# Decode attention, forward and backward: the output projection's load moved back in the load queue

## The chip, the cores and the metric

The kernel runs on one core of one Trainium2 chip. The metric is the device time of one execution in microseconds (us); smaller is better. "Before" and "after" are the kernel without and with the change.

## The reference

The program computes a small transformer block for two decode tokens and all its gradients. Cut to what matters, with B = 2 batches, H = 32 heads, 4096 cached keys of 128 numbers per head, and a model width of 640, all in bf16:

```
q   = layernorm(x) @ wq                     # 640 -> 32 heads x 128
p   = softmax(q . K / sqrt(128))            # per batch and head, over 4096 keys
o   = p @ V
h   = x + concat(o) @ wo                    # 4096 -> 640
out = h + relu(layernorm(h) @ w1) @ w2      # 640 -> 1728 -> 640
# and from grad_out: the gradients of x, K, V, wq, wo, w1, w2
```

The K and V caches are 2 x 32 tiles of 1 MB each, and the gradients of K and V have the same sizes and are written out. These 1 MB tiles are nearly all of the traffic; wo is 5 MB, wq 5 MB, w1 and w2 2 MB each.

## The kernel before, in words

**Two sweeps.** The first sweep (`p1_iter`, L463) goes through the 64 pairs of batch and head in order. In iteration i it transposes K tile i on TensorE (L416), copies the transposed groups out of PSUM, and takes the scores (L427). In the next iteration it finds the softmax's maximum (L517, L519) and exponentials (L526) for tile i and multiplies them into K (`pk_half`, L478). In the one after that it multiplies the result with V tile i (`m_part`, L471) and sums it over the keys (`u_part`, L500). So iteration i reads K tile i, K tile i-1 and V tile i-2. The second sweep (`p2_iter`, L834) reads V once more and writes the gradients of K and V, each as an outer product on VectorE (L829) that GpSimd's queue stores (L867, L886). From iteration 41 of the first sweep on, one iteration of the second sweep runs beside every second one of the first.

**Between the sweeps.** When the first batch's 32 heads are through, `middle_gen` (L730) is queued as background work at iteration 33. It finishes the output projection, runs the second layer norm, multiplies with w1 (`hf_ps`, L755), goes back through the MLP with w1 on VectorE (L789), and takes the gradient of the attention's output with wo on VectorE (`go_group`, L670). Pieces of it are woven into the first sweep's iterations. The second sweep needs its results.

**The output projection** runs in groups of four heads, eight groups for a batch. `o_group` (L593) normalises four heads' outputs on VectorE. `a_group` (L600) multiplies them with their rows of wo in 20 small TensorE matmuls (L606) and adds the result up on VectorE (L608). `a_heads(i)` (L611) is called once in each iteration, before step 5, and does one of the two: the product of a group that is normalised, or else the normalising of the next group, when its heads are through and, for the first batch, when the quarter of wo that it needs was queued at least four iterations before (L617). What is left at iteration 33 is done by `middle_gen`.

**The load queue.** All loads of the first sweep are issued by SyncE in one fixed order. It is written out before the kernel runs: for each iteration, in this order, a piece of wq (every sixth), K tile i, V tile i-2, a tile of the second sweep, and then what the two lists name for it: `W_AT` the four quarters of wo and w1 (`load_weights`, L344), `W2_AT` the three pieces of w2:

```python
W_AT = (10, 15, 20, 24, 35)
W2_AT = (8, 13, 18)
...
if ii in W_AT:
    queue.append(("w", W_AT.index(ii)))
```

`pump` (L1097) takes entries from the head of this queue as long as there is a buffer. K, V, wq and w2 come into twelve buffers of 1 MB; wo and w1 have homes of their own and need none. A load that takes over a buffer is issued when the last reader of the old tile is done. SyncE issues in order, so nothing passes an entry that waits. The queue runs some iterations ahead of the work, as far as the buffers go. V tiles of the last six heads of the first batch stay in their buffers for the second sweep.

The order on each engine is fixed when the program is built. TensorE, too, works strictly in order, so a product that waits for its weights holds up all that stands behind it.

Of the kernel before, what the change touches and what calls it, by code (L numbers as in the profile page):

```python
# [15 lines left out]
def kernel(  # L16
# [23 lines left out]
    _, H, Sk, Dh = A_k_cache.shape  # L40
# [14 lines left out]
    OG = 4  # L55
# [337 lines left out]
    NP1 = len(pairs)  # L393
# [193 lines left out]
        yield  # L587


    o_next = [0]  # L590
    a_next = [0]

    def o_group():  # L593
        b, g = divmod(o_next[0], H // OG)
        hs = slice(g * OG, g * OG + OG)
        nc.vector.tensor_tensor(out=OU[:, b, hs], in0=OU[:, b, hs], in1=rt[:, b, hs], op=ALU.mult)
        nc.vector.tensor_copy(out=OFc[:, hs, b], in_=OU[:, b, hs])
        o_next[0] += 1

    def a_group():  # L600

        b, g = divmod(a_next[0], H // OG)
        a_ps = pst([128, ND], FP32, "mid", "a_ps")
        for c in range(ND):
            for h in range(g * OG, g * OG + OG):
                nc.tensor.matmul(a_ps[:, c:c + 1], lhsT=wo_t[:, h, c * 128:(c + 1) * 128], rhs=OFc[:, h, b:b + 1],  # L606
                                 start=(h == g * OG), stop=(h == g * OG + OG - 1))
        nc.vector.tensor_tensor(out=asum[:, b, :], in0=asum[:, b, :], in1=a_ps[:], op=ALU.add)  # L608
        a_next[0] += 1

    def a_heads(i):  # L611

        if a_next[0] < o_next[0]:
            a_group()
        elif o_next[0] < NP1 // OG and i >= o_next[0] * OG + OG + 2:
            b, g = divmod(o_next[0], H // OG)
            if b > 0 or i >= W_AT[g * OG * 4 // H] + 4:  # L617
                o_group()

    def u_out(b):  # L620
# [447 lines left out]
    i = j = 0  # L1068
# [7 lines left out]


    queue = []
    W_AT = (10, 15, 20, 24, 35)
    W2_AT = (8, 13, 18)  # L1080
    for n, (ii, jj) in enumerate(plan):
        if ii is not None:
# [7 lines left out]
        if ahead is not None and ahead < NP1 and turns[ahead] not in kept and ("W", ahead) not in queue:  # L1090
            queue.append(("W", ahead))
        if ii in W_AT:
            queue.append(("w", W_AT.index(ii)))
        if ii in W2_AT:
# [35 lines left out]
    for n, (i, j) in enumerate(plan):  # L1130
# [58 lines left out]
        for k, _ in enumerate(p1_iter(i, i < H + 1, 0)):  # L1189
            for _ in range(at.get(k, 0)):  # L1190
                if g2 is not None:
                    p2_step()
            if k == 5:
                a_heads(i)
            pump()

            spread[0] = 1 if i < P2_AT else 2
            at_k[0] = k
            if i >= P2_AT:
                slot[0] = int(k == 6 or (k == 1 and j is None))  # L1200
            elif i > H + 1:
                slot[0] = {1: 2, 3: 1, 4: 1, 6: 1}.get(k, 0)
            else:
                slot[0] = int(k in (1, 6))
            bg_step(0, rate)
            bg_step(1, 0.0)
# [43 lines left out]
```

## Time and profile before

| | |
|---|---|
| median of 4 runs | 918.41 us (915.03 to 921.66) |
| the profiled execution | 918.38 us, span of the profile 916.5 us |
| busy share of the span | PE 82%, DVE 76%, ACT 58%, POOL 18% |
| DMA | 363.00 MB, 394 to 396 GB/s over the span |
| granted TensorE clock, mean over the span | 0.781 |
| K, V tile loads: issue to landing, median | 14.4 and 14.3 us (1024 KB) |
| a quarter of wo: issue to landing, median | 19.8 us (1280 KB, 4 loads) |
| w1: issue to landing | 11.2 us (2160 KB, 1 load) |

The profile shows one execution. PE is TensorE, PEld its weight loads, DVE is VectorE, ACT ScalarE, POOL GpSimd, SP SyncE; a name with a q (SPq) is the engine's own instruction queue, which issues DMAs. L471 is line 471 of the kernel. In lines with a time in front, the first number is the start in us from the span's start and the second how long it took; a bracket at the end tells how long the engine stood idle before it and what ended that. The name `w_t` stands for w1 and for the pieces of w2, with their numbers left out; w1 is the one of 2160 KB, issued by L349.

### The profile page before, as it was taken

What the parts mean: (1) busy time and instruction counts of PE and PEld (TensorE: products, weight loads), DVE (VectorE), ACT (ScalarE), POOL (GpSimd) and SP (SyncE); (2) the same over time, 40 slices, a digit from 0 to 9 for tenths busy, and PEclk for the clock granted to TensorE, in tenths of its full rate; (3) what the DMA queues carried; (4) which work ended last, traced back from release to release, by engine and by line L of the source; (5) the groups of instructions that cost most, each with busy time, mean ns of one, the idle gap of its engine ahead of it and who ended that gap; (6) DMA issues with size and microseconds to landing.
All of it is one profiled execution on the core that took longest, in us unless ns stands there. A gap on an engine that the chain in (4) does not pass through costs nothing.

```text
span 916.5 us, 26502 instructions
## 1 busy us (share of the span) xinstructions
PE 750.4 (82%) x11226; PEld 627.7 (68%) x11226; DVE 692.7 (76%) x1291; ACT 531.4 (58%) x1096; POOL 166.0 (18%) x329
## 2 busy tenths in 40 slices
PE   5998898999989898988887946866878799878493
PEld 5887786888878787877776835754657567555362
DVE  4655785877778887777768789977798359998875
ACT  3665564566777776776643535544656667566362
POOL 1222222223201101010011112111122011111111
PEclk9999998999999999999885576556655556565556
DMA  8999999998889999999999999999999999999997
GB/s 346 418 395 411 406 393 410 411 417 336 309 320 326 412 422 422 422 423 422 410 360 410 368 424 405 398 410 394 398 406 386 424 368 423 425 426 425 425 422 315
DMA packets 59478, 363.00 MB, mean 396 GB/s; under 512 B 5696, under 2 KB 15552, under 8 KB 19168
## 3 DMA queue, kind: packets, MB, share of 16 engines
q1 hardware_dynamic: 37920, 212.18, 58.3%
q0 software_dynamic: 18432, 134.23, 35.3%
q10 hardware_dynamic: 3008, 14.91, 4.1%
q8 instruction: 88, 1.44, 0.6%
q14 instruction: 30, 0.25, 0.1%
HBM read 212.16 MB, written 149.13 MB: 394 GB/s over the span
## 4 chain that ended last, share of the span: by engine, by line
PE 38%; DMA 27%; DVE 18%; ACT 8%; issue 7%; POOL 1%; POOLq 0%; SPq 0%; ACTq 0%; DVEq 0%
DMA out_dram<-gK 13%; DMA Vt<-in_A_v_cache_dram 11%; PE t_ps L437 8%; PE m_ps L471 8%; PE t_ps L416 7%; DVE gV L829 5%; DVE gK L829 4%; ACT t_sb L421 4%; PE s_ps L427 3%; DVE junk L656 3%; PE o_ps L933 3%; PE u_ps L500 2%; DVE pk L478 2%; DVE gxj L656 2%; PE dp_ps L450 2%
## 5 line engine op out<-in xcount | busy, mean ns | idle before, releaser
L421 ACT COPY t_sb<-t_ps 128x1024 bf16<-128x1024 bf16 x223 | 217.5, 1017 | 45.8 <-PE t_ps L416 45.6
L442 ACT COPY t_sb<-t_ps 128x512 f32<-128x512 f32 x256 | 149.9, 588 | 148.3 <-PE t_ps L437 144.3
L437 PE MATMUL t_ps<-ident_f,Wt 128*128 128x128 f32 x848 | 199.5, 384 | 1.6 <-ACT t_sb L421 1.6
L478 DVE TENSOR_TENSOR pk<-Kt,ep 128x2048 bf16<-128x2048 bf16 x128 | 156.3, 1221 | 57.7 <-ACT ep L526 25.5
L471 PE MATMUL m_ps<-pk,Vt 128*128 128x129 bf16 x2048 | 171.5, 222 | 17.6 <-DMA Vt<-in_A_v_cache_dram 16.5
L829 DVE TENSOR_TENSOR gK<-rb,gsp 128x2048 bf16<-128x2048 bf16 x128 | 152.1, 1223 | 21.1 <-DMA out_dram<-gK 18.7
L829 DVE TENSOR_TENSOR gV<-rb,pp 128x2048 bf16<-128x2048 bf16 x128 | 152.7, 1218 | 16.9 <-DMA out_dram<-gV 7.8
L416 PE MATMUL t_ps<-ident_bf,Kt 128*128 128x128 bf16 x2048 | 153.6, 224 | 10.2 <-DMA Kt<-in_A_k_cache_dram 5.0
L471 PEld LDWEIGHTS <-Vt 128*128 128x128 bf16 x2048 | 125.1, 99 | 48.7 <-issue 30.5
L437 PEld LDWEIGHTS t_ps<-ident_f,Wt 128*128 128x128 f32 x848 | 138.2, 199 | 28.1 <-issue 21.7
L416 PEld LDWEIGHTS <-Kt 128*128 128x128 bf16 x2048 | 126.0, 100 | 18.0 <-issue 9.0
L450 PEld LDWEIGHTS <-t_sb 128*128 128x128 bf16 x2048 | 96.6, 107 | 39.4 <-ACT t_sb L442 18.2
L450 PE MATMUL dp_ps<-gom,t_sb 128*128 128x2 bf16 x2048 | 95.6, 168 | 8.9 <-ACT t_sb L442 8.2
L488 POOL COPY pk<-ep 128x16 bf16<-128x16 bf16 x80 | 62.7, 785 | 194.2 <-ACT ep L526 162.1
L427 PE MATMUL s_ps<-qc,t_sb 128*128 128x1 bf16 x2048 | 88.1, 164 | 1.2 <-DVE t_sb L419 1.2
L867 POOL DMA_DIRECT2D out_dram<-gK x64 | 34.0, 532 | 278.2 <-DVE gK L829 209.6
L886 POOL DMA_DIRECT2D out_dram<-gV x64 | 34.2, 534 | 267.4 <-DVE gV L829 221.6
L939 ACT CAST ot<-o_ps 128x512 bf16<-128x512 f32 (+4 forms) x160 | 70.4, 488 | 17.2 <-DMA out_dram<-ot 8.7
L427 PEld LDWEIGHTS <-t_sb 128*128 128x128 bf16 x2048 | 77.7, 97 | 3.7 <-DVE t_sb L419 1.3
L583 ACT CAST MT<-m_ps 128x128 bf16<-128x128 f32 x64 | 17.1, 267 | 76.3 <-PE m_ps L471 76.2
L856 ACT ACTIVATE rb<-dp_ps,rt 128x256 bf16<-128x256 f32 x64 | 30.4, 475 | 51.3 <-PE dp_ps L851 50.6
L656 DVE CUSTOM_DVE_ANT_0 junk<-wo_t,hbc 128x640 bf16<-128x640 bf16 x64 | 52.3, 818 | 0.2
(194 smaller groups left out, 775.0 us busy)
## 6 DMA issues: line engine op xcount, KB each, us to landing
Kt<-in_A_k_cache_dram SPq DMA_DIRECT2D x64, 1024.0 KB, 14.4
Vt<-in_A_v_cache_dram SPq DMA_DIRECT2D x64, 1024.0 KB, 14.3
out_dram<-gV POOLq DMA_DIRECT2D x64, 1024.0 KB, 10.9
out_dram<-gK POOLq DMA_DIRECT2D x64, 1024.0 KB, 10.6
Wt<-in_A_v_cache_dram SPq DMA_DIRECT2D x53, 1024.0 KB, 12.1
wo_t<-in_A_wo_dram SPq DMA_DIRECT2D x4, 1280.0 KB, 19.8
wqs<-in_A_wq_dram SPq DMA_DIRECT2D x5, 1024.0 KB, 14.2
wq_t<-in_A_wq_dram SPq DMA_DIRECT2D x5, 960.0 KB, 11.1
```

The source lines that it names most:

```text
L416: nc.tensor.transpose(t_ps[:, j, :], nat[:, g * GT + j, :], ident_bf[:])
L421: nc.scalar.copy(out=t_sb[:], in_=t_ps[:])
L427: nc.tensor.matmul(dst[:, sc:sc + 1], lhsT=t_sb[:, j, :], rhs=vec, start=True, stop=True)
L437: nc.tensor.transpose(t_ps[:, j, :], natf[:, 2 * cc:2 * cc + 2, :].rearrange("p c k -> p (c k)"), ident_f[:])
L442: nc.scalar.copy(out=t_sb[:], in_=t_ps[:])
L450: nc.tensor.matmul(dst[:, sc:sc + 2], lhsT=v[:, j, :, par], rhs=vecs[:, par, :], start=(par == 0), stop=(par == 1))
L471: nc.tensor.matmul(r["m"][:, 0:129], lhsT=r["V"][:, sc, :], rhs=r["pk"][sc // HALF][:, sc % HALF, 0:129], start=(sc == 0), stop=(sc == NSC ...
L478: nc.vector.tensor_tensor(out=p["pk"][k][:, :, 0:128].rearrange("p s (a two) -> p s a two", two=2), in0=p["K"][:, sl, :].rearrange("p s (a ...
L488: nc.gpsimd.tensor_copy(out=col, in_=e)
L656: nc.vector.tensor_tensor_reduce(out=junk[0:kc, 0:width], in0=in0, in1=in1, scale=1.0, scalar=0.0, op0=ALU.mult, op1=ALU.add, accum_out=acc)
L829: nc.vector.tensor_tensor(out=pairs_view(dst[:, sl, :]), in0=row.rearrange("p (a two) -> p a two", two=2)[:, None, :, :].to_broadcast([128 ...
L939: nc.scalar.copy(out=ot[0:P, k, n0:n0 + nn], in_=o_ps[0:P, 0:nn])
```

## The change

It touches two places. In the list `W_AT`, the quarters of wo are named for iterations 14, 19, 28 and 33 instead of 10, 15, 20 and 24, and w1, the list's last entry, for 36 instead of 35. In `a_heads`, the normalising of a group (`o_group`) is no longer the alternative to a product (`a_group`): both may now run in the same iteration, first the product of the group before, then the normalising of the next. And the first iteration in which a quarter's groups may be normalised is now named in a list of its own, `WO_HERE`, instead of four after the quarter's place in the queue (16, 21, 29 and 31, where it was 14, 19, 24 and 28).

```diff
+    WO_HERE = (16, 21, 29, 31)
     o_next = [0]
     a_next = [0]
...
         if a_next[0] < o_next[0]:
             a_group()
-        elif o_next[0] < NP1 // OG and i >= o_next[0] * OG + OG + 2:
+        if o_next[0] < NP1 // OG and i >= o_next[0] * OG + OG + 2:
             b, g = divmod(o_next[0], H // OG)
-            if b > 0 or i >= W_AT[g * OG * 4 // H] + 4:
+            if b > 0 or i >= WO_HERE[g * OG * 4 // H]:
                 o_group()
...
-    W_AT = (10, 15, 20, 24, 35)
+    W_AT = (14, 19, 28, 33, 36)
     W2_AT = (8, 13, 18)
```

## The prediction

> **What bounds the kernel now.** I call iteration i of the first sweep "row i": it transposes K tile i and uses V tile i-2. I read the page's slices first, then stretches of 10 to 20 us, then the chain, then the two queues that matter, TensorE and SyncE.
>
> ```profile
> PEclk9999998999999999999885576556655556565556
> DMA  8999999998889999999999999999999999999997
> ```
>
> The DMA engines are full nearly everywhere, with one dip in slices 10 to 13. Stretches show where it starts (columns: PE, PEld, DVE, ACT, POOL busy, clock, DMA share, GB/s):
>
> ```profile
> 20.00:40.00 20.00, 19.16 (x370) 16.77 (x370) 12.07 (x20) 12.35 (x24) 4.06 (x11) 1.00 1.01 418
> 60.00:80.00 20.00, 16.22 (x297) 13.52 (x295) 10.01 (x15) 10.51 (x21) 4.27 (x7) 0.94 1.02 406
> 140.00:160.00 20.00, 16.93 (x295) 14.56 (x299) 11.07 (x23) 9.99 (x19) 4.98 (x7) 0.83 1.02 409
> 210.00:220.00 10.00, 9.74 (x191) 8.33 (x189) 6.00 (x9) 7.07 (x13) 3.89 (x5) 1.00 0.78 294
> 240.00:250.00 10.00, 8.79 (x176) 7.77 (x172) 9.90 (x25) 8.36 (x17) 1.61 (x4) 1.00 0.68 237
> 300.00:320.00 20.00, 17.64 (x330) 15.78 (x330) 16.81 (x28) 15.53 (x33) 2.77 (x4) 1.00 1.01 420
> ```
>
> Up to 210 us loads and TensorE are neck and neck: the queue is full, and TensorE mostly has 19 of 20 us. From 210 to 290 the engines set the pace and the queue has gaps. From 300 to 880 DMA is at 0.97 to 1.01, with nothing in hand to make a delay good. TensorE's rows show where loads come late before 210:
>
> ```profile
> 76.22 0.64 PE L471 MATMUL m_ps<-pk,Vt 128*128 128x129 bf16 x8 [2.91 <-DMA Vt<-in_A_v_cache_dram]
> 110.04 0.64 PE L471 MATMUL m_ps<-pk,Vt 128*128 128x129 bf16 x8 [1.37 <-DMA Vt<-in_A_v_cache_dram]
> 141.57 1.15 PE L416 MATMUL t_ps<-ident_bf,Kt 128*128 128x128 bf16 x16 [2.79 <-DMA Kt<-in_A_k_cache_dram]
> 144.06 1.05 PE L471 MATMUL m_ps<-pk,Vt 128*128 128x129 bf16 x8 [1.23 <-DMA Vt<-in_A_v_cache_dram]
> ```
>
> These are rows 11, 16 and 21, each shortly behind a quarter of wo. The last places are w1's load on SyncE, its size and time to landing, and its first reader on TensorE:
>
> ```profile
> 215.64 0.44 SPq L349 DMA_DIRECT2D w_t<-in_B_w_dram  x1
> 220.30 0.33 SPq L458 DMA_DIRECT2D Kt<-in_A_k_cache_dram  x1
> 226.42 0.33 SPq L458 DMA_DIRECT2D Vt<-in_A_v_cache_dram  x1
> 226.85 0.37 SPq L458 DMA_DIRECT2D Kt<-in_A_k_cache_dram  x1
> ```
>
> ```profile
> w_t<-in_B_w_dram SPq DMA_DIRECT2D x1, 2160.0 KB, 11.2
> ```
>
> ```profile
> 226.36 1.05 PE L416 MATMUL t_ps<-ident_bf,Kt 128*128 128x128 bf16 x16
> 231.02 0.89 PE L755 MATMUL hf_ps<-x2c,w_t 128*128 128x1 bf16 x30
> ```
>
> w1 is issued at 215.64, lands at 226.83 and is read at 231.02, in row 35, which starts at 226.36. It has 4.2 us in hand.
>
> **Quarters 0 to 2 of wo.** Landings (by the trace's DMA semaphores) follow the order of issue: K and V tiles land 2.49 us apart (141.52 and 144.01 for K21 and V19), and a quarter lands 3.51 us after the load ahead of it in three of four cases (once 5.21). A row without waits takes 5.51 us (89.30 to 94.81); every fourth takes 0.20 more, one with a piece of q 0.76 more (row 5: 6.27), one with a wo product 0.50 more (row 25: 6.01). Rows 11 to 23 took 162.66-72.19 = 90.5 us against 13x5.51+3x0.20+3x0.76+4x0.50 = 76.5, so 14.0 us went to late loads and to the half clock behind them.
>
> Quarter 0 moves behind V12 (past eight tiles and a piece of w2), quarter 1 from behind V13 to behind V17, quarter 2 from V18 to V26, quarter 3 from V22 to V31. In row 11, V9 lands at 76.17-3.51 = 72.66, and TensorE wants it at 73.14: no wait. TensorE then reaches row 15 at 72.19+6.27+5.71+5.51+5.51 = 95.19. But K15 and V13 have quarter 0 ahead of them before and after the change, so they land when they did, at 98.93 and 101.50: 5.4 us of wait come back here. Row 15 goes on at 101.54, as before. With the slow clock behind it (1.9, below) row 16 starts at 101.54+4.56+1.9 = 108.0 (before 107.55). K16 and V14 now have one quarter fewer ahead: no wait. Rows 16 to 20 take 5.71+6.77+6.01+5.51+5.71 = 29.7, to 137.7. K21 and V19 have two quarters ahead instead of three and land at 138.0 and 140.5: waits of 0.3 and 1.5, and row 21's V products start at 140.5 instead of 144.06. The first gain is one quarter, 3.5 us, plus up to 1.8 if the shorter waits bring no slow clock.
>
> **Quarter 3** is wanted by the product in row 32. It lands behind V31: 209.91-3.51+3.51 = 209.9. TensorE comes there at 208.91-3.5-0.5+5.28 = 210.2 (one wo product fewer stands before row 32), or 208.4 with the 1.8 above: a wait of 0 to 1.5. The next row starts at 209.9+0.94 = 210.9 to 211.1, not 214.62. So the gain at row 33 is 3.5 to 3.8; I take 3.7. If the 5.21 us were the quarter's true price, quarter 3 would land at 208.2 and the gain be 5.5. If one of the odd landing gaps of 1.5 (V9 came 4.03 after K11, K30 4.04 after V27) fell badly, it would be 2.0.
>
> **Products in neighbouring rows.** The eight products of the first half stay eight: rows 15, 17, 20, 22, 25, 27, 31, 34 become 17, 18, 22, 23, 30, 31, 32, 34, each 0.50 us of TensorE. Their three VectorE operations (0.15 to 0.17 us) move along, and VectorE has 6 to 8 of 20 us free in most of these stretches: nothing. From row 33 on, the order on the compute engines is unchanged.
>
> **w1, the last entry of the list, goes from row 35 to 36.** That moves its load past K36 and V34. V34 waits for VectorE's second product with K33, at the end of row 34, and so issues at row 35's start (226.42 against 226.36). w1 can't issue before it: 226.85 on the old scale, 0.5 into row 35. With the measured 11.19 it lands at 238.0, and TensorE wants it at 231.02: 7.0 us of wait. Everything behind that weight load on TensorE waits too: the rest of row 35's V products and scores, hence the maximum on VectorE and the exponential on ScalarE, and the MLP's whole chain to row 41. No transfer uses the time, since the tiles behind w1 need buffers that these rows free. Lower bound: V36 to V38 landed 4.7 to 5.0 after issue from an empty queue; with 5.0, and w1's 640 packets of 135 ns on 16 engines (5.4 us) behind, it lands at 236.8, a wait of 5.8. Upper: V34 landed 5.59 after issue and w1 6.53 after the load ahead: 238.5, a wait of 7.5. I take 7.0, w1's own row.
>
> The page "DMA: Bandwidth & Descriptors" of the Trainium skill, section on the anatomy of one DMA, gives about 2.0 us plus bytes at 436 GB/s: for V34 and w1 together, 3.26 MB, I estimate 9.5 us from V34's issue, 235.9, a wait of 4.9, and the sum below would be 2.1 us lower. Its rules for kernel authors say to issue a load early and wait late, which speaks against moving w1.
>
> **The clock behind waits.** After row 11's wait the clock averages 0.57 over 77 to 81 us and 0.53 over 142 to 149. From row 11's V products to row 12 it took 6.34 us instead of 5.32, and row 12 lost 1.03 more (together 2.05); row 21 lost 1.76. Row 16's short waits cost none. So 0 to 2.05 behind w1's wait; I take 1.8, as it is the longest of these waits. The skill's page "TensorE: Matmul & The Clock Gate", part 1, has half rate after an idle window of about 3.4 us until one busy window has passed; by that alone I estimate 1.7.
>
> **Sum.** 7.0 + 1.8 - 3.7 = +5.1 us; with the bounds, 5.8+0-5.5 = +0.3 to 7.5+2.05-2.0 = +7.5. The profiled execution took 918.38 us (span 916.5, 1.9 around it), the median of four is 918.41, so the same base serves: 923.5, own range 918.7 to 925.9.
>
> **Rivals.** (a) The two sides nearly cancel: w1 waits 5.8, with little slow clock, and the early gain is 5.5, about +0.3 to +4.5: 918.7 to 922.9. For it: all three are within rows seen. Against: it needs more than one of them at its end.
> (b) Faster: the wait for w1 is made good later. That is so if the stretch from 290 us on is set by loads that don't depend on row 35; then only the early gain stays, -3.7 to -5.5, so 912.9 to 914.7. It decides at row 44, whose V42 landed at 291.93, with 1.0 us in hand before its products at 292.90: if V42 lands no later than before, the delay is gone. Against: V36 to V43 are each issued on a release by TensorE or VectorE, with 4.7 to 9.4 us to landing, so the queue isn't ahead.
> (c) Worse: quarter 3 lands late. SyncE once took 11.85 us to issue the load behind a quarter (50.96). If that holds back K34, issued near 194, to 206, it lands near 211 and is wanted at 216: no cost. If quarter 3 itself comes 3.5 late, the early gain is gone: +8.8, 927.2.
>
> **Numbers.** Half a per cent, 4.6 us, is about what a measurement of this kernel can tell from no change. My forecast, slower by more than that, has 0.48 with (c)'s 0.05 in it; (a) 0.39; (b) and any other gain 0.13. The range, 916 to 927, takes the own range, some of the spread of the runs before (915.03 to 921.66) on both sides, and leaves out (b) and the tail of (c).
>
> **What would show it.** Right: a TensorE wait of about 7 us on w1 before the first hf product, no wait in row 11, 5 us in row 15, row 21's V products near 140.5, row 33 near 211, row 37 some 4 to 5 later than 240.04. Wrong: no wait at w1, or row 44 where it was (291.96).

## Result, and the profile after

The changed kernel takes 920.7 us (median of 38 runs, 916.67 to 926.41), the kernel before 917.21 us (59 runs, 912.45 to 921.94). The ratio is 1.0041, 95% interval 1.0028 to 1.0053, or +3.8 us (2.6 to 4.9); the two medians themselves differ by 3.5. The interval lies above 1, so the change is slower, and by less than the half per cent that the prediction called no change.

The profiled execution of after took 918.89 us (span 917.0), only 0.5 more than that of before (918.38). The profiled ends are a poor measure here: the same kernel, run twice below (e7 and e11), stands 0.7 us apart at row 44 and 3.8 us apart in span. So each step is read from the traces up to row 44, near 292 us, and the total from the ratio of many runs.

The slices of after, clock and DMA share, answer to those of before:

```profile
PEclk9999899999799999897995775756757555565556
DMA  9999999997788999999999999999999999999997
```

The 8 that the clock had in slice 7 (137 to 160 us) is gone; there is an 8 in slice 5, where row 15 waits, and a 7 in slice 11 (229 to 252 us), where before had a 9. The dip of the DMA row, 888 in slices 10 to 12, is now 7788 in slices 10 to 13. The stretches of 10 to 20 us (PE, PEld, DVE, ACT, POOL busy, clock, DMA share, GB/s) show the two sides of the change:

```profile
20.00:40.00 20.00, 19.62 (x357) 17.56 (x356) 11.27 (x19) 12.26 (x23) 4.97 (x9) 0.92 1.01 419
60.00:80.00 20.00, 19.61 (x400) 17.46 (x398) 11.97 (x21) 12.18 (x25) 4.62 (x9) 1.00 1.01 416
140.00:160.00 20.00, 19.61 (x427) 17.48 (x425) 15.01 (x34) 11.00 (x24) 6.21 (x10) 1.00 1.01 416
210.00:220.00 10.00, 10.00 (x188) 9.47 (x185) 5.18 (x16) 7.14 (x15) 2.71 (x3) 0.83 0.77 288
240.00:250.00 10.00, 9.90 (x184) 8.63 (x183) 7.83 (x17) 8.27 (x16) 3.12 (x5) 0.93 0.39 133
300.00:320.00 20.00, 17.52 (x326) 15.14 (x323) 17.14 (x33) 15.35 (x32) 3.94 (x5) 1.00 0.99 405
```

The first and the last line lie ahead of and behind the stretch that the change touches and differ little; the 0.92 in the first can't come of the change, since the two kernels issue the same loads up to 50 us. From 60 to 80 and from 140 to 160 us TensorE now does 19.6 of 20 us at the full clock, where it did 16.2 and 16.9 at 0.94 and 0.83. From 210 to 220 and from 240 to 250 us the clock is at 0.83 and 0.93, where it was 1.00. From 240 to 250 us the DMA share falls from 0.68 to 0.39: by then the tiles behind w1 wait for buffers, as predicted (V36's load for 9.2 us, until 246.08).

TensorE's rows (start, us, engine, line, operation, tiles, and in brackets the idle time ahead and its releaser) at rows 15, 21, 32, 33 and 35:

```profile
98.98 1.89 PE L416 MATMUL t_ps<-ident_bf,Kt 128*128 128x128 bf16 x16 [3.18 <-DMA Kt<-in_A_k_cache_dram]
101.48 1.05 PE L471 MATMUL m_ps<-pk,Vt 128*128 128x129 bf16 x8 [0.50 <-DMA Vt<-in_A_v_cache_dram]
139.77 0.64 PE L471 MATMUL m_ps<-pk,Vt 128*128 128x129 bf16 x8 [1.34 <-DMA Vt<-in_A_v_cache_dram]
209.49 0.65 PE L607 MATMUL a_ps<-OFc,wo_t 128*128 128x1 bf16 x20 [1.46 <-DMA wo_t<-in_A_wo_dram]
210.44 1.61 PE L416 MATMUL t_ps<-ident_bf,Kt 128*128 128x128 bf16 x16
223.37 1.05 PE L416 MATMUL t_ps<-ident_bf,Kt 128*128 128x128 bf16 x16
233.74 0.96 PE L756 MATMUL hf_ps<-x2c,w_t 128*128 128x1 bf16 x30 [5.54 <-DMA w_t<-in_B_w_dram]
```

Row 21's V products stand at 139.77 instead of 144.06, row 33 at 210.44 instead of 214.62: 4.2 us ahead. The wait in row 32 is quarter 3 of wo landing at 209.44. Row 33 then runs at half clock (210.7 to 214.2) and takes 6.70 us, not 5.51, so that row 35 is 3.0 ahead (223.37 against 226.36). Its first hf product then waits 5.54 us for w1. Row 33 of before, row 44 of before and row 44 of after start so:

```profile
214.62 1.05 PE L416 MATMUL t_ps<-ident_bf,Kt 128*128 128x128 bf16 x16
291.96 1.05 PE L416 MATMUL t_ps<-ident_bf,Kt 128*128 128x128 bf16 x16
296.65 1.05 PE L416 MATMUL t_ps<-ident_bf,Kt 128*128 128x128 bf16 x16
```

SyncE's queue shows why w1 is late:

```profile
217.30 0.33 SPq L458 DMA_DIRECT2D Kt<-in_A_k_cache_dram  x1
223.42 0.33 SPq L458 DMA_DIRECT2D Vt<-in_A_v_cache_dram  x1
223.80 0.43 SPq L349 DMA_DIRECT2D w_t<-in_B_w_dram  x1
224.33 0.47 SPq L458 DMA_DIRECT2D Kt<-in_A_k_cache_dram  x1
```

Both tiles ahead of w1 waited for a buffer: K36 for 8.2 us behind V33, and V34 for 6.1 us more, up to the start of row 35. w1 stands 0.38 behind V34. V34 lands at 228.27, w1 at 233.69. The list of waits (engine, line, releaser: us in total, times, longest) puts the same wait at 5.7 us on the weight load, and the stretch behind it shows the clock:

```profile
PEld L756 <- DMA w_t<-in_B_w_dram: 5.7, 1, 5.7
```

```profile
230.00:240.00 10.00, 6.26 (x115) 6.24 (x116) 1.07 (x6) 1.77 (x4) 0.00 (x0) 0.56 1.01 402
```

The clock is half of full from 231.2 to 241.5. Row 35 takes 14.06 us instead of 7.51, row 36 takes 7.63 instead of 6.17. Row 37 starts at 245.06 instead of 240.04, and row 44 at 296.65 instead of 291.96, 4.7 later.

### The profile page after: what moved, and what is told of

Its sections match the earlier page's. It is cut to its first block, busy times and chain, and to the rows that moved or that the text cites. A ratio compares the mean times of both kernels' runs of the same rounds, so it can differ in the third digit from the quotient of the medians.

```text
span 917.0 us, 26501 instructions
## 1 busy us (share of the span) xinstructions
PE 739.8 (81%) x11226; PEld 618.5 (67%) x11226; DVE 693.2 (76%) x1291; ACT 530.8 (58%) x1096; POOL 169.6 (18%) x329
## 4 chain that ended last, share of the span: by engine, by line
PE 35%; DMA 30%; DVE 18%; ACT 9%; issue 6%; POOL 1%; SPq 0%; POOLq 0%; ACTq 0%; DVEq 0%
DMA Vt<-in_A_v_cache_dram 9%; PE m_ps L471 8%; PE t_ps L416 7%; PE t_ps L437 7%; DMA out_dram<-gV 6%; DMA out_dram<-gK 6%; DVE gV L830 5%; DMA wqs<-in_A_wq_dram 5%; ACT t_sb L421 4%; DVE gK L830 3%; PE s_ps L427 3%; DVE pk L478 3%; DVE junk L657 2%; PE u_ps L500 2%; DVE gxj L657 2%
## 5 line engine op out<-in xcount | busy, mean ns | idle before, releaser
L437 PE MATMUL t_ps<-ident_f,Wt 128*128 128x128 f32 x848 | 189.1, 368 | 1.4 <-ACT t_sb L421 1.4
L416 PE MATMUL t_ps<-ident_bf,Kt 128*128 128x128 bf16 x2048 | 156.1, 226 | 10.0 <-DMA Kt<-in_A_k_cache_dram 4.6
L437 PEld LDWEIGHTS t_ps<-ident_f,Wt 128*128 128x128 f32 x848 | 131.0, 191 | 31.3 <-issue 25.5
L416 PEld LDWEIGHTS <-Kt 128*128 128x128 bf16 x2048 | 128.4, 101 | 17.7 <-issue 9.7
L450 PEld LDWEIGHTS <-t_sb 128*128 128x128 bf16 x2048 | 93.0, 105 | 40.9 <-ACT t_sb L442 20.6
L427 PEld LDWEIGHTS <-t_sb 128*128 128x128 bf16 x2048 | 77.9, 97 | 4.7 <-ACT t_sb L421 1.2
```

The lines of the kernel that those rows point to most:

```text
L416: nc.tensor.transpose(t_ps[:, j, :], nat[:, g * GT + j, :], ident_bf[:])
L427: nc.tensor.matmul(dst[:, sc:sc + 1], lhsT=t_sb[:, j, :], rhs=vec, start=True, stop=True)
L437: nc.tensor.transpose(t_ps[:, j, :], natf[:, 2 * cc:2 * cc + 2, :].rearrange("p c k -> p (c k)"), ident_f[:])
L450: nc.tensor.matmul(dst[:, sc:sc + 2], lhsT=v[:, j, :, par], rhs=vecs[:, par, :], start=(par == 0), stop=(par == 1))
```

## The experiments

Each edit below is against after unless it says otherwise; `WO_HERE` sets from which iteration a quarter's first group may be normalised, and the group's product follows one row later. The two theories: by Theory 1 the total is the sum of the early gain and w1's delay, and row 44's shift stays to the end; by Theory 2 loads set the time behind row 44, and w1's delay is made good there.

**e1_w1_back: the quarters moved, w1 not.**

```diff
-    W_AT = (14, 19, 28, 33, 36)
+    W_AT = (14, 19, 28, 33, 35)
```

> The change with w1 at row 35 again, all else as after. Theory 1 (two terms: the quarters' move gains, w1's move costs): in after, row 35 starts at 223.37 instead of 226.36, a gain of 3.0 us, and row 44 starts at 296.65 instead of 291.96, so w1's move costs 7.7 up to there. Without it the first TensorE read of w1 waits for nothing, row 44 starts near 289, and the time is 3.0 under before: 914.2, ratio 0.997. Theory 2 (the delay at w1 is made good later, as the two profiled spans differ by 0.5 only, and the time comes from somewhere behind row 44): the time stays where after is, near 920 to 921, ratio 1.003 to 1.005.

Measured: 913.84 us, ratio 0.9984 (0.9956 to 1.0011). Row 35 starts at 223.19, w1 has landed at 224.62, and TensorE's first product with it has no wait:

```profile
209.31 0.65 PE L607 MATMUL a_ps<-OFc,wo_t 128*128 128x1 bf16 x20 [1.36 <-DMA wo_t<-in_A_wo_dram]
227.85 0.89 PE L756 MATMUL hf_ps<-x2c,w_t 128*128 128x1 bf16 x30
```

Row 44 starts at 289.64, 7.0 earlier than in after and 2.3 earlier than in before. So w1's one place costs 7.0 there, and 5.2 in the time (the ratio is 0.0057 below after's). Against before, the interval of e1 holds 1, so a gain of the time is not shown here. The quarters alone bring less than their 4.2 at row 33: row 33 still runs at half clock behind a wait (210.1 to 213.5), and the half clock comes once more, with no wait right ahead of it. A stretch of e1:

```profile
231.00:234.00 3.00, 3.00 (x31) 3.00 (x29) 0.73 (x5) 2.13 (x4) 0.00 (x0) 0.50 1.01 404
```

and the same stretch of before:

```profile
231.00:234.00 3.00, 3.00 (x97) 2.96 (x95) 1.30 (x3) 0.44 (x3) 1.29 (x2) 1.00 1.01 366
```

TensorE is busy throughout in both, at 0.50 in e1 and 1.00 in before.

**e2_w1_alone: the other half, against before.**

```diff
-    W_AT = (10, 15, 20, 24, 35)
+    W_AT = (10, 15, 20, 24, 36)
```

> Before with w1 at row 36, nothing else. Theory 1: a wait of 6 to 7 us ahead of the first hf product, the slow clock behind it, row 44 some 7.7 us later than 291.96, the time 7.7 over before: 924.9, ratio 1.008. Theory 2: the wait is there, the time is not more than 2 us over before.

Measured: 923.79 us, ratio 1.0078 (1.0055 to 1.0101), +7.2 us. w1 is issued at 226.53 and lands at 236.34:

```profile
236.40 0.96 PE L755 MATMUL hf_ps<-x2c,w_t 128*128 128x1 bf16 x30 [5.47 <-DMA w_t<-in_B_w_dram]
```

Row 44 starts at 299.35, 7.4 later than in before. The 7.4 at row 44 are 7.2 in the time, against Theory 2.

**e3_products_alone: neighbouring rows allowed, no load moved.**

```diff
-    WO_HERE = (16, 21, 29, 31)
+    WO_HERE = (14, 19, 24, 28)
...
-    W_AT = (14, 19, 28, 33, 36)
+    W_AT = (10, 15, 20, 24, 35)
```

> The edit of a_heads alone: a product and the next normalising in one iteration, with the old places of the loads and quarters' groups free from rows 14, 19, 24 and 28 as before. Theory 1: the same eight products of 0.5 us each, so no change: 917.2, within 2 us. Theory 3 (products in neighbouring rows press TensorE, or ease it, at the wrong places): a difference of over 2 us either way.

Measured: 916.64 us, ratio 0.9995 (0.9973 to 1.0018); the products stand in rows 15, 16, 20, 21, 25, 27, 31 and 34. Row 44 starts 1.2 earlier (290.73), but no difference in the time can be told.

**e4_w1_before_v34: w1 as late in the list, but not behind V34's wait for a buffer.**

```diff
-    W_AT = (14, 19, 28, 33, 36)
+    W_AT = (14, 19, 28, 33)
...
+        if ii == 36:
+            queue.append(("w", 4))
```

The two added lines stand between the entries of K36 and V34.

> The change, but in row 36 w1 stands between K36 and V34 instead of behind V34. Theory 1, in the form that it is V34's wait for its buffer that holds w1 back, and not the length of the queue: w1 issues right after K36, at about 217.7, lands by 228 to 229, and is wanted at 228.0: a wait of 0 to 1 us, and the time is within 1.5 us of the kernel with w1 at row 35 (914 to 916). If the queue's length were the reason, the wait would still be 4 us or more and the time near 920.

Measured: 915.55 us, ratio 0.9989 (0.9965 to 1.0012). SyncE's queue and the first reader:

```profile
216.98 0.33 SPq L458 DMA_DIRECT2D Kt<-in_A_k_cache_dram  x1
217.36 1.05 SPq L349 DMA_DIRECT2D w_t<-in_B_w_dram  x1
223.10 0.33 SPq L458 DMA_DIRECT2D Vt<-in_A_v_cache_dram  x1
```

```profile
230.27 0.96 PE L756 MATMUL hf_ps<-x2c,w_t 128*128 128x1 bf16 x30 [2.40 <-DMA w_t<-in_B_w_dram]
```

w1 is issued 6.4 us earlier than in after, but lands only 3.5 earlier, at 230.22: 12.9 us after its issue and 7.45 behind K36, not 5.4. The wait is 2.40; I had put it at 0 to 1. V34's wait for its buffer thus holds w1's issue back by 6.4 us. It is not the whole price. K36 waits for a buffer too, so w1 is issued at 217.36 here and at 209.23 in e1, where it stands ahead of both. Row 44 starts at 292.82, 0.9 later than in before: of the 7.0 us between after and e1, 3.8 go when w1 stands ahead of V34, and the other 3.2 only when it stands ahead of K36 too. Why w1 needed 7.45 us behind the tile ahead, no run shows.

**e5_product_later: e1, and quarter 3's first product one row later.**

```diff
-    WO_HERE = (16, 21, 29, 31)
+    WO_HERE = (16, 21, 29, 32)
...
-    W_AT = (14, 19, 28, 33, 36)
+    W_AT = (14, 19, 28, 33, 35)
```

> The change with w1 at row 35, and quarter 3's first group normalised from row 32 on, so that its product stands in row 33 and not in row 32, where it waited 1.46 us for the quarter. Theory 1: the product finds its quarter, the 1.46 us and the slow clock behind it (row 33 took 6.7 instead of 5.5) go, row 35 starts near 220.5 instead of 223.2, and the time is some 2.7 under the kernel with w1 at row 35 alone: near 912, ratio 0.995. If the half clock near 231 in that kernel, where TensorE had not waited, is a sequel of row 32's wait, it goes too and 1.2 more is won. Rival: the next loads in the queue, K34 to V33, are late by as much, and row 35 stays near 223.

Measured: 912.91 us, ratio 0.9949 (0.9927 to 0.9972). TensorE's rows for the product, row 35 and the hf product:

```profile
213.38 0.64 PE L607 MATMUL a_ps<-OFc,wo_t 128*128 128x1 bf16 x20
220.56 1.05 PE L416 MATMUL t_ps<-ident_bf,Kt 128*128 128x128 bf16 x16
225.22 0.89 PE L756 MATMUL hf_ps<-x2c,w_t 128*128 128x1 bf16 x30
```

The product has no wait, the half clock at 210 us is gone, and row 35 starts 2.64 us earlier than in e1; row 44 starts at 287.10, 2.5 earlier. A half clock from 228.4 to 231.8 remains (row 36 takes 7.46 us), so it is no sequel of the wait in row 32.

**e8_product_later_w1_36: the same product edit with w1 left at 36.**

```diff
-    WO_HERE = (16, 21, 29, 31)
+    WO_HERE = (16, 21, 29, 32)
```

> The change as it is, w1 at row 36, with the first product of quarter 3 in row 33. Theory 1: without row 32's wait row 35 starts near 220.5; the wait for w1 stays at 5 to 6 us with its slow clock, since w1 follows V34 and V34 the start of row 35: the time is 7 to 8 over the kernel with both edits, ratio 1.002 to 1.003, and 2 to 3 under the change. Rival (the wait for w1 is shorter or longer according to what the queue holds): a difference from the kernel with both edits outside 5 to 9 us.

Measured: 919.54 us, ratio 1.0027 (1.0006 to 1.0048). Row 35 starts at 220.84, 2.5 earlier than in after, and w1 waits all the same, since its issue moves with the row:

```profile
231.38 0.96 PE L756 MATMUL hf_ps<-x2c,w_t 128*128 128x1 bf16 x30 [5.70 <-DMA w_t<-in_B_w_dram]
```

Row 44 starts at 294.12, 7.0 later than in e5, and the ratio is 0.0078, 7.2 us, above e5's: a third reading of w1's price.

**e6_q2_q3_alone: quarters 0 and 1 where before had them.**

```diff
-    WO_HERE = (16, 21, 29, 31)
+    WO_HERE = (14, 19, 29, 31)
...
-    W_AT = (14, 19, 28, 33, 36)
+    W_AT = (10, 15, 28, 33, 35)
```

> Quarters 0 and 1 where they were before (rows 10 and 15), quarters 2 and 3 at 28 and 33 as in the change, w1 at row 35. Theory 1 (what counts is how many quarters stand ahead of V19): the waits in rows 11 and 16 are back, the one in row 15 is gone, V19 has two quarters ahead as in the change, and row 21's V products start near 140; row 35 starts near 223 and the time is that of the kernel with w1 at row 35 alone, ratio 0.998. Rival (the places of quarters 0 and 1 bring the gain): row 21's V products start near 144, ratio 1.000.

Measured: 912.88 us, ratio 0.9958 (0.9932 to 0.9984). Row 21's V products come at 140.81 with no wait, though the early waits are spread over rows 11, 14, 15 and 16 now (0.77, 0.76, 2.03 and 2.68 us; I had expected none in row 15). Row 35 starts at 222.12 and row 44 at 288.62, no later than in e1 (289.64). What counts for the early gain is how many quarters stand ahead of V19, two here as in after; moving quarters 0 and 1 as after does adds nothing.

**e7_spread, and again as e11_spread_again: quarters 0 and 1 later still.**

```diff
-    WO_HERE = (16, 21, 29, 31)
+    WO_HERE = (20, 25, 29, 32)
...
-    W_AT = (14, 19, 28, 33, 36)
+    W_AT = (18, 23, 28, 33, 35)
```

> As the kernel with the product in row 33 and w1 at row 35, with quarter 0 at row 18 (behind V16) and quarter 1 at row 23 (behind V21). Theory 1: K15 and V13 land 3.5 earlier, the wait of row 15 falls from some 3.7 to under 2; row 19 then waits some 2 for V17; V19 has one quarter ahead and lands near 136. From row 28 on the queue is no shorter than without this, so most of it is given back: row 35 starts 0 to 1.5 earlier than with quarters 0 and 1 at 14 and 19, ratio 0.993 to 0.995. Rival: with the load queue never ahead, each row waits a little and the slow clock comes more often: row 35 later than without, ratio 0.997 or more.

> The kernel with quarters at rows 18, 23, 28 and 33 once more, on one chip with the next one. By the traces its row 44 starts at 287.18, 4.8 us before that of the kernel before (291.96), and the one with quarter 2 at row 30 starts it at 286.34. Theory 1 (what is won up to row 44 stays): ratio 0.993 to 0.996 here. If something behind row 44 gave it 0.9928: lower still, 0.993 or less.

Measured: 911.2 us, ratio 0.9928 (0.9900 to 0.9956), then 912.73 us, 0.9954 (0.9935 to 0.9974). In e7 row 15's waits fall to 1.23, others come in rows 19 and 21 (1.78 and 2.43), and row 29 takes 8.94 us, 3.2 more than its 5.76. Row 35 starts at 221.58, 1.0 later than in e5, where I had expected it up to 1.5 earlier; row 44 starts at 287.18, as in e5. There is no half clock near 230 us, and row 36 takes 6.17. The second execution of the same kernel differs: row 29 takes 5.76 and loses nothing, half clock stands in row 21 instead (134.7 to 141.5, row 21 takes 9.25 and not 7.22), row 35 starts at 220.39 and row 44 at 286.51. So where the half clock falls, and what one row loses by it, is not fixed by the kernel.

**e9_spread_q2_30, and again as e12_q2_30_again: quarter 2 later too.**

```diff
-    WO_HERE = (16, 21, 29, 31)
+    WO_HERE = (20, 25, 30, 32)
...
-    W_AT = (14, 19, 28, 33, 36)
+    W_AT = (18, 23, 30, 33, 35)
```

> Quarters at rows 18, 23, 30 and 33, w1 at 35, products in rows 21, 22, 26, 27, 31, 32, 33 and 34. With quarter 2 at 28, row 29 waited 2.1 us for V27 behind it, with a half clock behind that, 3.2 us in all. Theory 1 (a wait comes where a quarter stands ahead of a load that TensorE is close to, and a quarter two rows later meets a longer queue): V27 lands 3.5 earlier, K31 and V29 behind the quarter are wanted 1 to 2 us after they land, row 29's loss goes, row 35 starts near 218.5 instead of 221.6, ratio 0.990. Rival: the wait only moves to rows 31 to 34, row 35 stays within 1 us of 221.6 and the ratio at 0.993.

> The kernel with quarters at rows 18, 23, 30 and 33 once more. Theory 1: within 0.002 of the ratio of the kernel with quarter 2 at row 28, since their rows 44 lie 0.8 us apart; the 0.9965 against 0.9928 measured on two chips would be the spread of the measurement. Rival (the later quarter 2 costs something behind row 44): 0.003 or more above it again.

Measured: 913.51 us, ratio 0.9965 (0.9937 to 0.9993), then 912.67 us, 0.9951 (0.9930 to 0.9973); I had expected 0.990. On one chip e11 and e12 differ by 0.0003, so the 0.9928 of e7 against the 0.9965 of e9 was the spread of the measurement. Row 29 takes 5.77 us in e9, but as it took 5.76 in e11, its loss in e7 can't be put down to quarter 2's place. Row 35 starts 2.4 us earlier than in e7 (e12 against e11: 1.1), but row 44 only 0.8 earlier (0.4). TensorE's waits near w1 in e9:

```profile
224.92 0.90 PE L756 MATMUL hf_ps<-x2c,w_t 128*128 128x1 bf16 x30 [0.92 <-DVE pk L478]
229.89 0.64 PE L471 MATMUL m_ps<-pk,Vt 128*128 128x129 bf16 x8 [0.99 <-DMA Vt<-in_A_v_cache_dram]
```

The first wait is put down to VectorE's pk, but w1 landed at 224.87, 0.05 ahead of the product; V34 landed at 229.84, as close to its own. The loads are now the late ones: the gain of TensorE has run into the queue.

**e10_all_late: every quarter as late as its product allows.**

```diff
-    WO_HERE = (16, 21, 29, 31)
+    WO_HERE = (24, 27, 30, 32)
...
-    W_AT = (14, 19, 28, 33, 36)
+    W_AT = (22, 25, 30, 33, 35)
```

> As the one with quarters at 18, 23, 30, 33, with quarters 0 and 1 at rows 22 and 25. Theory 1: one quarter fewer ahead of V19, so rows 19 and 21 lose less, but every load up to K34 is the same work for the queue by row 33, so at most 1 us is left to win at row 35: ratio 0.988 to 0.991. Rival (quarters placed late always gain 3.5 us each): row 35 3 us earlier still, ratio 0.986 or less.

Measured: 913.71 us, ratio 0.9955 (0.9932 to 0.9978), row 35 at 219.24, row 44 at 286.23. That is nothing more than e9; I had expected 0.988 to 0.991.

Row 44's shift against the change of the time (ratio less 1, times before's 917.21), in us:

| kernel | row 44 | time |
|---|---|---|
| e2_w1_alone | +7.4 | +7.2 |
| after | +4.7 | +3.8 |
| e8_product_later_w1_36 | +2.2 | +2.5 |
| e4_w1_before_v34 | +0.9 | -1.0 |
| e3_products_alone | -1.2 | -0.5 |
| e1_w1_back | -2.3 | -1.5 |
| e6_q2_q3_alone | -3.3 | -3.9 |
| e5_product_later | -4.9 | -4.7 |
| e7_spread, e11_spread_again | -4.8, -5.5 | -6.6, -4.2 |
| e9_spread_q2_30, e12_q2_30_again | -5.6, -5.8 | -3.2, -4.5 |
| e10_all_late | -5.7 | -4.1 |

The shift reaches the end to within 2.5 us everywhere, from +7.4 to -5.8. Theory 2 falls. Seven runs of five kernels with w1 at 35 (e5 to e7, e9 to e12) beat both the kernel before and the changed one, at 0.993 to 0.997; their intervals overlap, so none of them is shown to be the best.

## Why the prediction was right, point by point

The forecast was +5.1 us, the runs give +3.8. The direction and the two terms were right, a gain in front and a larger cost at w1. The size came out smaller than the forecast, within half a per cent and so among the numbers of rival (a), and that the sum came as close as it did is in part luck, as the points below show.

- **First gain.** Confirmed, a little too small. No wait in row 11; row 15's V products at 101.48 (101.54 forecast), row 16 at 107.14 (108.0, so less slow clock), row 21's V products at 139.77 behind 1.34 of wait (140.5 and 1.5). The wait in row 15 was 3.68 us and not 5.4: half clock from 98.1 us on made the row's transposes longer (1.89 us against 1.05), and the V products came when V13 did all the same. e6 shows the working to be right in its core, one quarter fewer ahead of V19. It also shows that the moves of quarters 0 and 1, on which the prediction spent a paragraph, were not needed for it.
- **Quarter 3.** It landed at 209.44 (209.9), with a wait of 1.46 (0 to 1.5). Row 33 started 4.2 earlier (3.7). The step that was missing is what this wait does to the clock: 1.2 us of half clock in row 33. The product one row later takes wait and half clock away, 2.5 to 2.6 us at row 35 (e5 against e1, e8 against after). I had priced the wait and called a short one free, since row 16's short waits cost none. That was one execution: in e2, the same kernel up to row 34, half clock follows row 16's waits (107.7 to 111.2), and the row takes 7.44 us instead of 6.92.
- **Products in neighbouring rows.** Nothing was forecast, and e3 shows nothing in the time (0.9973 to 1.0018).
- **w1.** The mechanism was right: behind V34, 0.4 us into row 35 (0.5). The term was mis-sized: 5.54 on TensorE, 5.7 on its weight load, instead of 7.0, below the lower bound of 5.8. I took w1's own row of before, 11.19 us from issue to landing; here it was 9.89. Both are the rest of the tile ahead (V33 4.66 and V34 4.47 us after w1's issue) and w1's own time behind that tile, 6.53 in before and 5.42 in after. The lower bound's 5.4, worked out from packets, was the better price: eleven of the 14 traces here have 5.36 to 5.54. But e3 has 6.45, before 6.53 and e4 7.45, so that it is no safe price either.
- **w1's time by the page.** The page "DMA: Bandwidth & Descriptors" of the Trainium skill gave, by the section on the anatomy of one DMA, an estimate of 9.5 us for V34 and w1 from V34's issue. That section's formula is a fit to loads issued through GpSimd, and these two are SyncE's, so the prediction stretched it. This trace has 10.27, so the wait lay between that estimate's 4.9 and my 7.0, nearer to the 4.9.
- **The clock behind waits.** The half clock of 10.3 us cost 1.46 in row 36 and 0.85 in row 35 (14.06 less 7.51, less the wait of 5.7), 2.3 in all and not 1.8. Part of it is not the wait's: without any wait for w1, row 36 takes 7.46 in e5. The prediction's upper bound of 2.05 was also misread: 1.03 of it was row 12's, but row 12 takes 6.74 us in after too, with no wait and no half clock in row 11, and in before the half clock had ended at 81.0, ahead of row 12 (82.56). The largest loss seen in before was 1.76, and what followed w1's wait was more.
- **The sum at row 37.** +5.0 measured, 4 to 5 forecast. It is made of a gain of 3.0 at row 35 and w1's 5.7 + 2.3 = 8.0. Two misses cancelled, which is luck: w1 0.8 less than 7.0 + 1.8, the gain at row 35 0.7 less than 3.7. Of the 1.2 between this +5.0 and the +3.8 of the runs, 0.3 are gone by row 44; the rest is not traced to anything and lies inside the interval of 2.6 to 4.9.
- **Rivals.** (a) had three conditions, and only the first came: w1's wait was short, but the slow clock was not little (2.3) and the early gain was 3.0 at row 35, not 5.5. So the total is (a)'s without (a)'s reason. (b) is refuted: row 44 is 4.7 later and the end 3.8, and the table shows the same from +7.4 to -5.8. (c) did not happen: quarter 3 came on time. SyncE did take 8.93 us to issue K34 behind it (from 192.65), and K34 was not waited for.
- **Two readings on which nothing rested.** The dip of the DMA row in before is in slices 10 to 12, not 10 to 13. VectorE's free time in the stretches of 20 us from 60 to 200 us of before is 2.8 to 10.0 us, not 6 to 8 in most of them; by e3 the products' new rows cost nothing all the same.

**What stays open.** The half clock near 228 to 234 us in e1, e5 and e6, with no wait of TensorE right ahead of it, is absent in before and e7, and costs about 1.3 us in row 36. e5 shows that the wait in row 32 isn't its cause. The traces show what goes with it. In each trace all changes of the clock lie on one grid of 3.41 us, and the grid's offset differs from one execution to the next. Count in each step of the grid the columns that TensorE's products take in: 128 for a transpose, 129 for a V product, 1 for an hf product. Between 60 and 290 us the 14 traces have 899 steps at full clock. The 26 that half clock follows have 2999 columns or fewer; of the other 873 all but two have more. The step ahead of the half clock has 2665 columns in e1, 2908 in e5 and 2664 in e6, with TensorE busy throughout, since the one-column hf products fell into it; before's step with these products has 3283, and in e7 they are split over steps of 7363 and 4159. No run changes the columns alone, and behind 460 us, among other products, the count no longer separates the two kinds of step. So this is read off the traces and not tested, and what sets the clock stays open.

## What to carry to other kernels

A load moved one place in a queue can cost far more than that place's time, if the entry that it now follows waits for a buffer: ask what the new neighbour ahead waits for, and whether the load's first reader stands within its time to landing. Here one iteration's place in the list, past two tiles that each waited for a buffer, cost 7.0 to 7.4 us at row 44 (5.2 to 7.2 in the time) and ate a gain made by the other four moves. Price a load by the rest of the tile ahead and its own time behind it, with several rows for each, and not by one row's time from issue to landing. Where a product may wait a little for its load, put it one step later, because the slow clock behind the wait can cost as much as the wait. And read a row's loss to the slow clock from more than one execution.

## What the hardware showed that was not expected

A wait's length alone did not tell whether the half clock would follow. After 1.46 us in row 32 of after TensorE ran at half clock for 3.4 us; after 1.34 in row 21 the mean clock of 140 to 160 us was 1.00; in e1 and e5 half clock came without a wait. Counted by the grid's steps, as above, row 32's wait lies in a step of 2344 columns, and row 21's in steps of 4521 and 7837. After the 5.54 us wait for w1 half clock lasted until 241.5, 7.8 us past the wait's end, though TensorE had products all along: its three steps, mostly of hf's one-column products at first, have 288, 2233 and 3727 columns.

The page "TensorE: Matmul & The Clock Gate" of the Trainium skill, part 1, has half rate after an idle window of about 3.4 us until a busy one has passed, in windows that run freely. The half clock's length in row 32 and the grid of 3.41 us agree. That 1.46 us of wait were enough, or none at all, and that 7.8 us of products did not end it sooner, does not agree, if idle and busy mean TensorE's waits and products; there the measurement decides.

SyncE took 8.93 us to issue K34 behind quarter 3 (from 192.65), but the DMA engines stayed full over 195 to 210 us.
